# Twelfth slot of a fused top-k attention and gated MLP: diagonal matrices ahead of the last weight roundings, a later output copy, and seven buffers in two pools

## The chip, the cores and the metric

The kernel runs on one core of a Trainium2 chip. The metric is the device time of one launch in microseconds (us), as the median of several runs. Lower is better. The core has five engines with queues of their own: TensorE (PE, with its weight loads listed apart as PEld), VectorE (DVE), ScalarE (ACT), GpSimd (POOL) and SyncE (SP), which here only issues DMAs. Each works through its own list in the order in which the kernel wrote it; semaphores order the engines among each other.

## The reference

```python
# attention: q, k, v of shape (8, 8, 576, 64) = (B, H, S, D), top_k = 32
scores = (1.0 / np.sqrt(D)) * np.matmul(q, k.transpose(0, 1, 3, 2))
kth = np.partition(scores, -top_k, axis=-1)[..., -top_k:-top_k + 1]
scores = np.where(scores >= kth, scores, -1000000000.0)
attn = np.exp(scores - np.max(scores, axis=-1, keepdims=True))
attn = attn / (np.sum(attn, axis=-1, keepdims=True) + 1e-09)
x = np.matmul(attn, v)            # then (B, H, S, D) -> (B*S, H*D) = (4608, 512)
# MLP: w_in (512, 2048), w_out (2048, 512)
h = x @ w_in
g = h * (1.0 / (1.0 + np.exp(-1.702 * h)))
out = g @ w_out
```

The gate is computed as h times (1 + tanh(0.851 h)), with the factor one half applied when the output is copied.

## The kernel before, in words

**Tiles and slots.** A unit of attention is a slot: 128 query rows of two heads. A batch has 18 slots, so 8 batches make 144. Slots 0 to 12 are written one at a time by `slot(n)` (the constant `SETTLED` is 12), from slot 13 on `two_slots(n)` writes two at a time, and `last_slot()` drains what is left of the MLP. All orders are written out by hand under a manual schedule: an engine does what the Python code issued for it, in that order.

**One slot of attention.** `scores(n)` multiplies queries and keys on PE into the tiles `s_ps` (L282). `copy_scores(n)` brings them to SBUF as `sc` on ACT (L294). DVE then searches the 32 largest values of each row: with MAX8 and MATCH_REPLACE8 over 576 columns up to slot 11 (L304, L307), and from slot 12 on in two halves of 288 columns, `greater` and `lesser` (`pair_up`, L323 on DVE, L326 and L327 on POOL; `topk_of_pairs`, L344 to L356), which gives `cut`. `bounds(n)` makes `low` from it on POOL (L377). `exponentials(n)` masks and exponentiates on ACT (L397, L400). Up to slot 11 `divide(n)` then forms 1/sum on DVE (L408, L410) and, on POOL, two diagonal matrices `by` that hold it (L413; they lie in one place of the tensor `xT`). `turn_main` and `turn_ends` multiply the probabilities by these matrices on PE, so that they come out turned and divided (L448, L451), and ACT copies them to `pt` (L456). From slot 12 on ACT splits the probabilities into 16-bit halves (`split`, L470), SP writes them to DRAM (`rows`, L472) and brings them back with a transposing DMA (L478); sums are then divided out later through `wide` (L433) and L527. `values` (L503) or `values_at` (L538) multiplies by v, and ACT copies the result (L516, or `x` at L953 with L552 on POOL after it) to `xT`.

**The MLP beside it.** When 128 rows of `xT` are complete they make a block, and the MLP of the blocks runs in pieces between the attention's steps: `hidden()` multiplies by `win` on PE (L595), `tanh()` takes the hyperbolic tangent on ACT into a tile `th` (L617) and, from slot 13 on, also copies h (tile `h`, L620), `gate()` multiplies the two (on DVE at L632 up to slot 12, on POOL at L629 and L630 afterwards), and `project()` multiplies by `wout` on PE into `po` (L650). A block takes four `project()` calls with four matmul groups each. After the fourth, `leave` copies `po` to a tile `ob` on ACT (L658) and SP writes it out (L660). `project(True)` puts that copy off to the next `leave_all()`. The next block's first L650 has to wait until `ob` has been copied, because `po` is one buffer.

**Weights.** The 32 weight pieces arrive as 64-bit words and are turned into float32 in the first slots ("rounding"). SP loads a piece to a tile `raw` one slot ahead (L126), ACT and DVE prepare it (L151 to L154), and POOL ends it with two operations, L144 and L147. These two go to a list `unfinished` and are issued inside the next slot's search on DVE, by `finish_one()`: the first three after the third operation of the search, all that are left after the sixth, behind `divide`. Slot 11 prepares the last two pieces, so slot 12 issues four such operations.

```python
for i, op in enumerate(topk_of_pairs(n) if n >= PAIRED else topk(n)):
    op()
    if i == 2:
        for _ in range(min(3 if n >= TURNS else 6, len(unfinished))):
            finish_one()
    if i == 5:
        if n > 0:
            divide(n - 1)
        while unfinished:
            finish_one()
```

**Buffers.** The pool `raws` has 8 buffers of 4 KB a partition, and the tiles `raw`, `lesser`, `h`, `x` and `wide` take turns in it. The pool `thp` has 5 buffers of 2 KB, shared by `th` and `ob`. A tile is written only when the last reader of the tile that had the buffer before is done.

**From slot 12 to slot 13.** `slot(12)` ends with `project()` and `hidden()`. `two_slots(13)` (where `opens` is true) then issues `scores(15)`, `bring_all()` with a `hidden()`, `exponentials(12)`, `split(12)`, `copy_scores(15)`, a `tanh`, the search of slot 13, another `hidden`, `project_one()` and a second `tanh`.

Of the kernel before, what the change touches and what calls it, by code (L numbers as in the profile page):

```python
# [30 lines left out]
def kernel(  # L31
# [53 lines left out]
    SETTLED = 12  # L85
# [3 lines left out]

    const = ctx.enter_context(tc.tile_pool(name="const", bufs=1))  # L90
    pool = lambda name, bufs, **kw: ctx.enter_context(tc.tile_pool(name=name, bufs=bufs, **kw))
    raws = pool("raws", 8)
    loads = pool("loads", 2)
    vals = pool("vals", 4)
    qkt = pool("qkt", 6)
# [3 lines left out]
    small = pool("small", 4)  # L99
    ptp = pool("ptp", 2)  # L100
    xs = const.tile([P, 5, CC, P], F32, name="xT")
    thp = pool("thp", 5)
    apart = pool("apart", 4, space=DRAM)
    apart_qk = pool("apart_qk", 2, space=DRAM)
    ps_s = pool("ps_s", 2, space=PSUM)
# [506 lines left out]
    def tanh(aside):  # L612

        if to_gate:
            ph, g, blocks = to_gate.pop(0)
            th = thp.tile([P, G * P], F32, name="th")
            nc.scalar.activation(th[:], ph[:], AF.Tanh, scale=0.851 / RAISE)  # L617
            if aside:
                h = raws.tile([P, G * P], F32, name="h", tag="raw")
                nc.scalar.copy(out=h[:], in_=ph[:])  # L620
                ph = h
            gated.append((th, ph, g, blocks))
# [14 lines left out]
    def project(put_off_leaving=False):  # L637

        gT, fs, blocks = to_project.pop(0)
        for x in blocks:  # L640
            if not x.done:
                home = "ps_h" if "ps_p" in in_use else "ps_p"
                in_use.append(home)
                x.home = home
                pool_of, tag = (ps_h, "ph") if home == "ps_h" else (ps_p, "po")
                x.po = pool_of.tile([P, C], F32, name="po", tag=tag)
        i = 0
        for f in fs:
            for x in blocks:
                nc.tensor.matmul(  # L650
                    x.po[:], lhsT=gT[:, i * P : (i + 1) * P], rhs=wout[:, f, :], start=(x.done == 0), stop=(x.done == FC - 1)
                )
                x.done += 1
                i += 1

        def leave(x):
            ob = thp.tile([P, C], F32, name="ob", tag="th")
            nc.scalar.mul(out=ob[:], in_=x.po[:], mul=0.5 / RAISE**2)  # L658
            for on, to in x.rows:
                nc.sync.dma_start(to, ob[on, :])  # L660

        for x in blocks:
            if x.done == FC:
                in_use.remove(x.home)
                leaving.append(lambda x=x: leave(x))
        if not put_off_leaving:
            leave_all()
# [4 lines left out]
    def leave_all():  # L672
        while leaving:
            leaving.pop(0)()
# [116 lines left out]
    def slot(n):  # L791

        todo = later.pop(n, [])
        for fn, args in todo:
            if fn is not prepare and fn is not prepare_by_dma:
                fn(*args)
        preparing = [(fn, args) for fn, args in todo if fn is prepare or fn is prepare_by_dma]
        some = [round_piece(x) for x in by_slot.get(n, [])] if n else early
        if n == 0:
            for piece in some:  # L800
                piece["low"]()
                piece["sign"]()
        else:
            bounds(n - 1)
            if n == PAIRED:
                pair_up(n)

            exponentials(n - 1, bring_all if n % 4 == 1 else lambda: None)
            copy_scores(n + 1)
            bring_all()  # L810
            while signs:
                signs.pop(0)()
            if 1 < n <= TURNS:
                turn_main(n - 2)
                turn_ends(n - 2)
            for piece in some:
                piece["size"]()
            tanh(False)
        for i, op in enumerate(topk_of_pairs(n) if n >= PAIRED else topk(n)):
            op()  # L820
            if i == 2:
                for _ in range(min(3 if n >= TURNS else 6, len(unfinished))):
                    finish_one()
            if i == 5:
# [4 lines that stand above are left out]
            if i == 10:  # L829
                gate(False)  # L830
        for piece in some:
            piece["shift"]()
            unfinished.extend(piece["finish"])
        if n < NP:
            for fn, args in preparing:
                fn(*args)
        if n >= TURNS:
            turn_main(n - 1)
            turn_ends(n - 1)
        if n > 0:  # L840
            for piece in some:
                piece["low"]()
        scores(n + 2)
        if n == SETTLED:
            copy_scores(n + 2)
        if n == 0:
            return
        for i, piece in enumerate(some):
            if n == TURNS and i > 0:
                signs.append(piece["sign"])  # L850
            else:
                piece["sign"]()
        idle = not ready and n < TURNS
        if 1 < n <= TURNS:
            values(n - 2, put_off if n == TURNS else None)
        if n >= TURNS:
            values(n - 1, put_off)
        if n >= NP:
            for fn, args in preparing:
                fn(*args)  # L860
        if n > PROJECTS and may_project(2):
            project()
        if idle:
            stay_warm(8)
        hidden()
# [12 lines left out]
    def two_slots(n):  # L878

        first, second = [later.pop(m, []) for m in (n, n + 1)]  # L880
        live = lambda m: 0 <= m < N
        aside = n < N

        def begin(todo):
            for fn, args in todo:
                if fn is not prepare and fn is not prepare_by_dma:
                    fn(*args)

        def prepare_some(todo):
            for fn, args in todo:  # L890
                if fn is prepare or fn is prepare_by_dma:
                    fn(*args)

        def find(m):
            for i, op in enumerate(topk_of_pairs(m) if live(m) else [lambda: None] * 23):
                op()
                if i == (13 if m < SETTLED + 4 else 8) and m % 2:
                    invert(m - 2)
                if i > 1 and unfinished:
                    finish_one()  # L900

        def project_one():
            if may_project(0):
                project(True)

        def measure(m):
            if live(m):
                bounds(m)
            gate(aside)

        opens = n == SETTLED + 1
        ahead = n < SETTLED + 4
        begin(first)
        measure(n - 1)
        if ahead:
            scores(n + 2)
        if opens:
            bring_all()
        if live(n - 1):
            exponentials(n - 1)  # L920
            split(n - 1)
        if ahead:
            copy_scores(n + 2)
        if opens:
            tanh(aside)
        find(n)
        hidden(ps_t if opens else None)
        project_one()
        tanh(aside)
        prepare_some(first)  # L930
        held = [m for m in (n - 3, n - 2) if live(m) and "rows" in st[m]]
        o = ps_t.tile([P, 2, 2, P], F32, name="o", tag="tp") if held else None
        for i, m in enumerate(held):
            sum_rows(m, o[:, i, 0, :])
        if live(n + 2) and not ahead:
            scores(n + 2)
            copy_scores(n + 2)
        leave_all()
        for i, m in enumerate(held):
            values_at(m, o[:, i, 1, :])  # L940
        if live(n - 1):
            turn_by_dma(n - 1)
        while turns:
            turns.pop(0)()
        if live(n + 3):
            scores(n + 3)
        begin(second)
        measure(n)
        def bring():
            if not held:  # L950
                return
            x = raws.tile([P, 2, 2, P], F32, name="x", tag="raw")
            nc.scalar.copy(out=x[:], in_=o[:])  # L953
            for i, m in enumerate(held):
                x_of(m, x[:, i, 1, :], x[:, i, 0, :])

        if live(n):
            exponentials(n, bring)
        else:
            bring()  # L960
        if live(n):
            split(n)
            turn_by_dma(n)
        hidden(ps_t)
        if live(n + 3):
            copy_scores(n + 3)
        tanh(aside)
        prepare_some(second)
        project_one()
        leave_all()  # L970
        find(n + 1)
# [39 lines left out]
```

## Time and profile before

| what | value |
|---|---|
| median of 3 runs | 1477.44 us (1475.12 to 1478.23) |
| the profiled execution, its own time | 1475.54 us |
| its span in the profile | 1473.8 us |
| PE busy | 1433.5 us (97%) |
| DVE busy | 1333.4 us (90%) |
| ACT busy | 1173.9 us (80%) |
| POOL busy | 862.9 us (59%) |

The span runs from the first to the last instruction that the profiler saw; some 1.7 us of the execution's own time lie around it. Times of instructions are given from the span's start. A busy PE is modelled, so PE's share says where it has gaps and not how good its work is. In a row of the timeline the columns are start, length, engine, line, operation, output and inputs, shapes and count; a bracket at its end gives the idle time before it and what ended it. A row of waits reads: who waited, for whom, us in total, number of times, longest.

### The profile page before, as it was taken

What the parts mean: (1) busy time and instruction counts of PE and PEld (TensorE: products, weight loads), DVE (VectorE), ACT (ScalarE), POOL (GpSimd) and SP (SyncE); (2) the same over time, 40 slices, a digit from 0 to 9 for tenths busy, and PEclk for the clock granted to TensorE, in tenths of its full rate; (3) what the DMA queues carried; (4) which work ended last, traced back from release to release, by engine and by line L of the source; (5) the groups of instructions that cost most, each with busy time, mean ns of one, the idle gap of its engine ahead of it and who ended that gap; (6) DMA issues with size and microseconds to landing.
All of it is one profiled execution on the core that took longest, in us unless ns stands there. A gap on an engine that the chain in (4) does not pass through costs nothing.

```text
span 1473.8 us, 29103 instructions
## 1 busy us (share of the span) xinstructions
PE 1433.5 (97%) x9696; PEld 1017.8 (69%) x9696; DVE 1333.4 (90%) x4541; ACT 1173.9 (80%) x1865; POOL 862.9 (59%) x1119
## 2 busy tenths in 40 slices
PE   7789899999999999999999999999999999999998
PEld 5667656777666667777666667777666667777665
DVE  7999899999999999999999999999999999999910
ACT  6998687978788887888878787888878788887730
POOL 3777655665666666566665666655666666655510
PEclk8899999999999999999999999999999999999999
DMA  7451256877767677676768686666776766654430
GB/s 244 134 156 55 56 157 180 213 176 177 176 187 198 169 187 188 178 191 162 187 177 204 168 187 184 183 183 170 182 186 185 199 170 187 153 126 128 125 86 15
DMA packets 516311, 242.04 MB, mean 164 GB/s; under 512 B 452672, under 2 KB 490560, under 8 KB 516160
## 3 DMA queue, kind: packets, MB, share of 16 engines
q1 hardware_dynamic: 515728, 239.89, 62.1%
q8 instruction: 76, 1.25, 0.4%
q14 instruction: 75, 0.61, 0.1%
q10 hardware_dynamic: 432, 0.30, 0.1%
HBM read 45.09 MB, written 102.24 MB: 100 GB/s over the span
## 4 chain that ended last, share of the span: by engine, by line
PE 89%; DVE 5%; ACT 3%; issue 2%; DMA 1%; POOL 0%; POOLq 0%; ACTq 0%; SPq 0%
PE ph L595 33%; PE po L650 32%; PE s_ps L282 10%; PE o L538 10%; DVE top L304 3%; DVE left L307 2%; PE tp L448 1%; PE o L527 1%; ACT pr L400 1%; ACT sc L397 0%; ACT sc L294 0%; PE o L503 0%; DMA pt<-rows 0%; PE none L169 0%; DVE win L152 0%
## 5 line engine op out<-in xcount | busy, mean ns | idle before, releaser
L595 PEld LDWEIGHTS ph<-xT,win 128*128 128x128 f32 x3520 | 484.1, 191 | 86.8 <-issue 57.5
L595 PE MATMUL ph<-xT,win 128*128 128x128 f32 (+1 forms) x3520 | 537.6, 309 | 1.4 <-POOL xT L552 1.2
L650 PE MATMUL po<-wout,th 128*128 128x512 f32 x1152 | 518.4, 593 | 1.1 <-ACT ob L658 1.1
L650 PEld LDWEIGHTS po<-wout,th 128*128 128x128 f32 x1152 | 213.2, 190 | 214.5 <-issue 207.4
L344 DVE MAX8 top<-left 128x8 f32<-128x288 f32 x792 | 325.3, 445 | 0.0
L470 ACT COPY sc<-pr 128x2304 uint16<-128x2304 uint16 x132 | 278.8, 2112 | 4.2
L294 ACT ACTIVATE sc<-s_ps 128x576 f32<-128x576 f32 x288 | 171.1, 646 | 137.0 <-PE s_ps L282 133.6
L552 POOL TENSOR_TENSOR xT<-x 128x128 f32<-128x128 f32 (+1 forms) x148 | 60.5, 432 | 296.7 <-ACT x L953 296.7
L347 DVE MATCH_REPLACE8 left<-top,left 128x288 f32<-128x288 f32 x528 | 229.7, 442 | 0.0
L400 ACT ACTIVATE pr<-sc,low 128x576 f32<-128x576 f32 x288 | 221.4, 778 | 0.0
L326 POOL TENSOR_TENSOR lesser<-sc,greater 128x576 int32<-128x576 int32 x132 | 186.4, 1412 | 58.0 <-DVE greater L323 57.3
L344 DVE MAX8 top<-lesser 128x8 f32<-128x288 f32 x528 | 213.7, 445 | 0.0
L397 ACT ACTIVATE sc<-sc,cut 128x576 f32<-128x576 f32 x288 | 208.2, 779 | 3.4 <-POOL cut L388 3.3
L327 POOL TENSOR_TENSOR lesser<-lesser,sc 128x576 int32<-128x576 int32 x132 | 186.6, 1414 | 10.4
L282 PE MATMUL s_ps<-qk_t 64*128 64x288 f32 (+1 forms) x1280 | 183.1, 433 | 0.2 <-ACT qk_t L218 0.2
L630 POOL TENSOR_TENSOR th<-th,h 128x512 f32<-128x512 f32 x128 | 163.7, 1279 | 10.8 <-POOL th L629 0.2
L629 POOL TENSOR_SCALAR th<-th 128x512 f32<-128x512 f32 x128 | 80.0, 625 | 125.4 <-ACT th L617 125.3
L323 DVE TENSOR_TENSOR greater<-sc 128x576 f32<-128x576 f32 x132 | 101.6, 770 | 48.2 <-ACT sc L294 47.5
L538 PE MATMUL o<-pt,v_l 128*64 128x128 f32 (+1 forms) x2368 | 143.6, 265 | 0.2 <-DMA pt<-rows 0.2
L538 PEld LDWEIGHTS o<-pt,v_l 128*64 128x64 f32 x2368 | 119.7, 137 | 25.7 <-issue 22.1
L282 PEld LDWEIGHTS s_ps<-qk_t 64*128 64x128 f32 (+1 forms) x1280 | 99.6, 178 | 41.4 <-issue 22.7
L617 ACT ACTIVATE th<-ph 128x512 f32<-128x512 f32 x144 | 86.0, 597 | 50.8 <-PE ph L595 43.4
(83 smaller groups left out, 1461.6 us busy)
## 6 DMA issues: line engine op xcount, KB each, us to landing
rows<-sc SPq DMA_DIRECT2D x132, 576.0 KB, 3.1
qk_rows<-halves SPq DMA_DIRECT2D x48, 256.0 KB, 2.8
qk_l<-in_q_dram SPq DMA_DIRECT2D x64, 128.0 KB, 3.0
raw<-in_moe_w_in_dram SPq DMA_DIRECT2D x16, 512.0 KB, 4.9
v_l<-in_v_dram SPq DMA_DIRECT2D x32, 256.0 KB, 3.3
raw<-in_moe_w_out_dram SPq DMA_DIRECT2D x16, 512.0 KB, 3.4
out_dram<-ob SPq DMA_DIRECT2D x32, 256.0 KB, 2.8
qk_l<-in_k_dram SPq DMA_DIRECT2D x62, 128.0 KB, 2.8
```

What stands on the lines that cost most here:

```text
L282: nc.tensor.matmul(ps[i][rows, c, 0:HALF], lhsT=qT[b, hps[p]][on, cols], rhs=kT[b, hps[p]][on, FIRST[i] + c * HALF : FIRST[i] + (c + 1) * ...
L294: nc.scalar.mul(out=to, in_=ps[i][:, :, 0:HALF], mul=SCALE)
L326: nc.gpsimd.tensor_tensor(out=whole, in0=a.bitcast(I32), in1=greater[n][:].bitcast(I32), op=ALU.subtract)
L327: nc.gpsimd.tensor_tensor(out=whole, in0=whole, in1=b.bitcast(I32), op=ALU.add)
L344: nc.vector.max(found(r, i, True), src[:, i, :])
L347: nc.vector.match_replace(to[:, i, :], found(r, i), src[:, i, :], LOWEST)
L397: nc.scalar.activation(sc[:, i, :], sc[:, i, :], AF.Prelu, bias=cut[:, i : i + 1], alpha=HUGE)
L400: nc.scalar.activation(pr[:, i * S : (i + 1) * S], sc[:, i, :], AF.Exp, bias=low[:, i : i + 1], accum_out=den[:, i : i + 1],)
L470: nc.scalar.copy(out=halves, in_=pr[:].bitcast(U16).rearrange("p (k h) -> p h k", h=2))
L538: nc.tensor.matmul(o[j * D : (j + 1) * D, cols], lhsT=main[:, j, c, :] if c < NF else tail[:, j, :], rhs=pt[:, MAIN[j] + c if c < NF else ...
L595: nc.tensor.matmul(ph[:, i * many * P : (i + 1) * many * P], lhsT=win[:, c, f * P : (f + 1) * P], rhs=xs[:, first : first + step * (many - ...
L650: nc.tensor.matmul(x.po[:], lhsT=gT[:, i * P : (i + 1) * P], rhs=wout[:, f, :], start=(x.done == 0), stop=(x.done == FC - 1))
```

## The change

Five edits. The pool `raws` gets 7 buffers in place of 8, and `thp` 7 in place of 5, so the SBUF that the two take together stays the same (32 and 10 KB a partition before, 28 and 14 KB after). In slot 12 no rounding operation is issued after the third operation of the search, so all four follow after the sixth, behind `divide(11)` and its two L413. In slot 12 `project()` puts its output copy off. And in `two_slots(13)` a `leave_all()` ahead of the first `tanh` issues that copy, now behind `exponentials(12)`, `split(12)` and `copy_scores(15)`; its DMA (L660) on SP so comes behind the DMA of `rows` for slot 12 (L472). No operation is added or removed, and PE and DVE keep their order.

```diff
-    raws = pool("raws", 8)
+    raws = pool("raws", 7)
...
-    thp = pool("thp", 5)
+    thp = pool("thp", 7)
...
-            if i == 2:
+            if i == 2 and n < SETTLED:
                 for _ in range(min(3 if n >= TURNS else 6, len(unfinished))):
                     finish_one()
...
         if n > PROJECTS and may_project(2):
-            project()
+            project(n == SETTLED)
...
         if opens:
+            leave_all()
             tanh(aside)
```

Lines from L925 on have a number that is higher by one after the change (L953 becomes L954).

## The prediction

> **What bounds the kernel now.** I read the page's shares first, then its slices, then the chain, then the stretch around slot 12 engine by engine.
>
> ```profile
> span 1473.8 us, 29103 instructions
> PE 1433.5 (97%) x9696; PEld 1017.8 (69%) x9696; DVE 1333.4 (90%) x4541; ACT 1173.9 (80%) x1865; POOL 862.9 (59%) x1119
> PE   7789899999999999999999999999999999999998
> PE 89%; DVE 5%; ACT 3%; issue 2%; DMA 1%; POOL 0%; POOLq 0%; ACTq 0%; SPq 0%
> ```
>
> PE is the bound but for the first slices. The table of stretches makes it sharper:
>
> ```profile
> 232.00:1387.00 1155.00, 1154.82 (x7760) 813.45 (x7762) 1100.45 (x3904) 956.63 (x1453) 707.10 (x927) 1.00 0.69 178
> ```
>
> (Columns: stretch, length, busy PE, PEld, DVE, ACT, POOL, granted clock, DMA share, GB/s.) From 232 to 1387 us PE idles 0.18 us, while DVE has 54.6 us to spare. So what ends earlier before 232 us can end the kernel earlier by as much, and gaps elsewhere on PE hardly exist. Up to slot 11 DVE is the bound (9.97 busy in nearly each 10 us); the change hardly touches that part. What is left is the stretch from 146 to 232 us. On PE, POOL and ACT it reads:
>
> ```profile
> 141.34 1.95 PE L448 MATMUL tp<-xT,pr 128*128 128x128 f32 x16
> 145.96 3.84 PE L595 MATMUL ph<-xT,win 128*128 128x128 f32 x32
> 153.58 3.68 PE L448 MATMUL tp<-xT,pr 128*128 128x128 f32 x16 [3.77 <-POOL xT L413]
> 159.97 3.70 PE L650 MATMUL po<-wout,th 128*128 128x512 f32 x8
> ...
> 149.27 1.29 POOL L144 TENSOR_TENSOR wout<-wout,raw 128x512 int32<-128x512 int32 x1
> 150.64 1.28 POOL L147 TENSOR_TENSOR wout<-wout,raw 128x512 f32<-128x512 f32 x1
> 151.88 1.29 POOL L144 TENSOR_TENSOR wout<-wout,raw 128x512 int32<-128x512 int32 x1
> 153.14 1.23 POOL L413 TENSOR_SCALAR xT<-ident,rden 128x128 f32<-128x128 f32 x2
> ...
> 163.71 0.60 ACT L658 ACTIVATE ob<-po 128x512 f32<-128x512 f32 x1 [3.69 <-PE po L650]
> 175.66 0.60 ACT L617 ACTIVATE th<-ph 128x512 f32<-128x512 f32 x1 [4.14 <-PE po L650]
> 176.78 0.66 PE L217 MATMUL tp<-ident,qk_l 128*128 128x128 f32 x4 [0.73 <-ACT h L620]
> ```
>
> PE has nothing from 149.81 to 153.58: it waits for the first diagonal matrix, which stands on POOL behind three roundings. DVE had delivered 1/sum at 149.62 (L410, 149.45 plus 0.17). When PE starts again, L448 takes 3.68 us where slot 11 took 1.95:
>
> ```profile
> 154.00:155.00 1.00, 1.00 (x7) 0.50 0.00 0
> 155.00:156.00 1.00, 1.00 (x6) 0.50 0.00 0
> 157.00:158.00 1.00, 1.00 (x10) 0.98 0.00 0
> ```
>
> (Stretch, length, PE busy, granted clock.) The clock is halved until about 157 us.
>
> **What the Trainium skill says.** "TensorE: Matmul & The Clock Gate", Part 1: The HAM clock gate, has PE fall to half its clock after an idle window of about 3.4 us and recover after about as long a busy one. The trace agrees: 3.77 us idle, then 0.50 for some 3 us; the 1.86 us gap at 224.5 left the clock at 1.00. "SBUF — State Buffer", SBUF: two separate sides, has DVE operations with two SBUF inputs and POOL take turns at a shared port. It fits the second L413 here (883 ns beside a DVE L323, other L413 some 375 ns); I use 0.72 us for the pair, as in slot 10. "Perfetto Trace Analysis", Optimization Strategy, reads the same gap repeating as a lack of buffers; here the th wait comes only three times (4.14, 1.53, 1.22 us, all between 171 and 195 us).
>
> **The change part by part.**
>
> *Roundings behind L413.* POOL ends L327 of slot 12 at 149.32, and would start L413 at 149.8 (1/sum at 149.62 plus the 0.17 us that the same step takes in slot 11: 138.44 to 138.61). The first matrix is there at 150.15, the second at 150.5. PE, free at 149.81, starts L448 at 150.2: gain 153.58 - 150.2 = **3.4 us**. A gap of 0.4 us leaves the clock up, so L448 takes 1.95 instead of 3.68: **1.7 us** more. L451, L282 and L503 follow as in slot 11 (0.3 us of slack for the ACT copies L456 there), and L650 starts near 154.9 instead of 159.97. It is the user of the last two pieces: the four roundings take 5.3 us in sum and end at 150.5 + 5.3 = 155.8 instead of 155.62. Of the four matmul groups (0.9 us each) that start at 154.9, the third reads piece 30 (done by 153.2) and the fourth, at 157.6, piece 31. Price zero, covered by 1.8 us. The next on POOL, L326 for slot 13, is 0.2 us later; DVE reads it at 162.93, 4 us after it is ready.
>
> *Output copy put off.* Now ACT stands 3.69 us for `po` at 160 us with L516, L397, L400 and L470 of slot 12 queued behind. After the change L516 follows values(11) at 155, L397 can go when `cut` is there (DVE L356, 156.9), L400 when `low` is (POOL, about 159.1; now 158.95), so L400 ends at 160.7, L470 at 162.9, L294 of slot 15 at 164.0 and `ob` at **164.5** (lengths 1.5, 2.1, 1.1, 0.6 from the rows now). Who waits for `ob`: PE's next L650, which follows L282 (158.6) and 64 L595 (159.8 to 167.1) and so starts at 167.1 instead of 172.02. Slack 2.6 us, price zero; if the cover were gone it costs what ACT is late. SP: `rows` of slot 12 goes out near 162.9, L660 waits for `ob` to 164.5 behind it, and the transposing L478 waits for `rows` (2.8 us now) to 165.7 anyway. Nothing is delayed there.
>
> *Seven th buffers.* The three waits of ACT L617 for L650 go. Each held `h`, and thereby the PSUM buffers that L217 and L221 need: PE gaps of 0.73 (176.06) and 0.78 us (195.2). Not all of that goes, since L221 waits for the ACT copy of the first half anyway, as it would some 0.2 us without it: **0.5 + 0.6 = 1.1 us**. From ACT's side nothing is late next: it is done with L620 near 168.3, PE needs the buffer at 170.7.
>
> *Seven raw buffers.* SP may load piece i when piece i-7 is rounded, instead of i-8. The trace gives both ends: piece 27 would be loaded at 105.95 instead of 102.31, lands 3.4 us later at 109.4 and is read by L151 at 116.37. Over all pieces the least slack is 6.7 us, also for the v and k loads queued behind on SP. From slot 13 on, a pair of slots takes six buffers (wide, lesser, h, x, h, lesser) in about 19 us; going back seven, the tightest reader is DVE's last read of a `lesser` (254.7), whose buffer the `h` near 264 gets. 9 us of slack, price zero.
>
> **Does the gain last?** Up to 180 us DVE is continuously busy and can't move; its results of slots 12 to 14 (156.9, 165.8, 174.7) come before ACT's new times by 2 us or more except the first, counted above. Then DVE's waits for ACT, 1.14 + 2.85 us at 180 to 184.5 and 1.20 us at 200.5, are what it can give; it moves up 5.2 us. ACT is the bound from 199.5 to 227 (the chain runs through L400, L470, L294, L397 there), and starts when PE has done L538: now 199.5, then 193.3. The cuts of slots 16 to 22 have 2.5 us or more in hand before ACT (slot 19: 227.06 against 229.60), so DVE moving up 1 us less than PE does no harm. L595 starts at 231.93 less 6.2. Behind it PE is full and DVE has about 1 us a pair to spare.
>
> Sum: 3.4 + 1.7 + 1.1 = **6.2 us**; I take 6.0 for small waits not seen. The span would be 1467.8 and that execution 1475.54 - 6.0 = 1469.5. The median of runs lies 1.9 us above that execution, so 1477.44 - 6.0 = **1471.4**.
>
> **Bounds of what is not shown.** L413 with port conflict: 0.4 us later. No warm clock: 1.7 lost. Waits of th not the cause of the PE gaps: 1.1 lost; gone whole: 0.4 gained. Some ACT slack gained in 157 to 199 us could also shorten ACT's own stretch: up to 1.4 us more gain (its wait at 198.1). Gain from 3 to 8 us.
>
> **Rivals.**
> - *The put-off copy becomes the wait.* If slot 12's exponentials keep their place at 164.35 (because POOL gives `low` late), `ob` ends at 171.0, L650 waits from 167.1, and 3.9 of 6.3 us are given back: gain 2.4, 1475.0. Against it: `low` of slot 12 comes at 158.95 even now.
> - *The lead is eaten.* ACT is 91% busy and DVE 94% between 199 and 232 us; if either sets its own start, the gain is 0 to 1 us: 1477. Against it: `x` (L953) at 199.52 waits 1.37 us for PE, and DVE has 5.2 us of waits before.
> - *Weights come late: slower.* One raw buffer fewer delays each third piece. It decides if a piece takes over 10 us (3.4 median and 6.7 slack; the longest of the trace was 8.3 to land). Then ACT, and DVE behind it, wait in slots 3 to 11, say 2 us in nine slots: 18 - 6 = 12 us slower, 1489. For it: SP already waits 19 times for roundings.
> - That the change doesn't act is hard to hold: in the built order both L413 stand directly behind L327, ahead of all four roundings, and `ob` behind L294.
>
> **Numbers.** Full gain 0.80, copy as wait 0.10, lead eaten 0.06, late weights 0.04. About 0.2% (3 us) can be told from no change. The first case is faster but for its lower edge (0.79), the second and third mostly within 0.2% (0.16), the last slower; I put 0.05 there for noise too. The likeliest alone is 1469.5 to 1473; the range of eight in ten, with the bounds and the second case, is 1469.0 to 1475.0.
>
> **What would show it.** In the profile after: L448 of slot 12 starts near 150.2 and takes 2 us, PE clock 1.00 there; L658 of slot 12 behind L470 near 164; no L617 waiting for L650; the first L595 after the b=1 pairs near 226 instead of 232; PE still without gaps behind it. I am wrong if PE waits for `ob` near 167, if SP holds a weight past its L151, or if gaps come after 226 us that take the lead back.

## Result, and the profile after

The changed kernel takes 1469.42 us (median of 4 runs, 1468.78 to 1470.06) against 1477.84 us before: ratio 0.9947, interval 0.993 to 0.9964, that is 7.8 us less by the ratio (5.3 to 10.3). A second comparison of the same two kernels gave 0.9962 (0.995 to 0.9975), 5.6 us less (3.7 to 7.4). The forecast was 6.0 us less, a median of 1471.4 us in a range of 1469.0 to 1475.0; the measured median stands near the lower edge of that range. The profiled execution took 1468.81 us, its span 1467.0.

Page of the kernel after: span, busy time, PE in 40 slices.

```profile
span 1467.0 us, 29219 instructions
PE 1430.7 (98%) x9696; PEld 1015.8 (69%) x9696; DVE 1336.3 (91%) x4541; ACT 1173.9 (80%) x1865; POOL 863.1 (59%) x1119
PE   7789989999999999999999999999999999999998
```

Timeline of the kernel after, PE, around slot 12 and at the head of PE's full stretch:

```profile
149.77 2.05 PE L448 MATMUL tp<-xT,pr 128*128 128x128 f32 x16 [1.24 <-POOL xT L413]
154.53 3.70 PE L650 MATMUL po<-wout,th 128*128 128x512 f32 x8
171.29 0.33 PE L221 MATMUL tp<-ident,qk_l 128*128 128x128 f32 x1 [0.24 <-ACT qk_t L218]
198.88 3.70 PE L650 MATMUL po<-wout,th 128*128 128x512 f32 x8 [1.13 <-ACT ob L658]
225.40 3.84 PE L595 MATMUL ph<-xT,win 128*128 128x128 f32 x32
```

The wait for the first diagonal matrix is 1.24 us instead of 3.77, L448 takes 2.05 us instead of 3.68, and the first L595 behind the attention-only stretch stands at 225.4 instead of 231.9. The same times on POOL and ACT:

```profile
149.34 0.72 POOL L413 TENSOR_SCALAR xT<-ident,rden 128x128 f32<-128x128 f32 x2 [0.54 <-DVE rden L410]
150.03 1.29 POOL L144 TENSOR_TENSOR wout<-wout,raw 128x512 int32<-128x512 int32 x1
```

```profile
163.59 0.60 ACT L658 ACTIVATE ob<-po 128x512 f32<-128x512 f32 x1
166.78 0.60 ACT L617 ACTIVATE th<-ph 128x512 f32<-128x512 f32 x1 [1.63 <-PE ph L595]
```

L413 now waits for DVE's 1/sum and no longer for roundings. `ob` is copied by 164.2, 2.4 us before PE's L650 at 166.58 needs `po` free, and L617 waits for its input, not for a th buffer. Table of stretches, after (in the second row the stretch of the same length that was shown of before):

```profile
154.00:155.00 1.00, 1.00 (x13) 0.66 (x10) 1.00 (x3) 0.85 (x3) 0.98 (x1) 1.00 0.00 0
226.00:1381.00 1155.00, 1154.85 (x7766) 813.25 (x7766) 1104.31 (x3909) 956.12 (x1452) 706.49 (x925) 1.00 0.69 178
```

The clock is whole, and PE stays full behind 226 us: instructions that were at 294 us and later all stand 6.71 us earlier, up to the last output copy (6.72).

Part of the 6.7 us is chance. In the profiled execution of before the clock was also halved in slot 8, where the change does nothing; in that of after it was not:

```profile
106.00:108.00 2.00, 2.00 (x11) 0.50 0.43 117
```

```profile
106.00:108.00 2.00, 2.00 (x19) 1.00 0.33 68
```

(Stretch, length, PE busy, clock, DMA share, GB/s; first before, then after.) In the execution of after PE then stands 1.27 us earlier in slot 11, and DVE's 1/sum for slot 12's matrices comes 0.45 us earlier (149.17 against 149.62). Less that, the profile shows some 6.3 us, an estimate.

### The profile page after: what moved, and what is told of

The parts are those of the page before. It is cut to its first block, busy times and chain, and to the rows that moved or that the text cites. A ratio compares the mean times of both kernels' runs of the same rounds, so it can differ in the third digit from the quotient of the medians.

```text
span 1467.0 us, 29219 instructions
## 1 busy us (share of the span) xinstructions
PE 1430.7 (98%) x9696; PEld 1015.8 (69%) x9696; DVE 1336.3 (91%) x4541; ACT 1173.9 (80%) x1865; POOL 863.1 (59%) x1119
## 4 chain that ended last, share of the span: by engine, by line
PE 82%; DVE 13%; ACT 2%; issue 1%; DMA 1%; SPq 1%; POOL 0%; POOLq 0%; DVEq 0%; ACTq 0%
PE ph L595 31%; PE po L650 30%; PE o L538 10%; PE s_ps L282 10%; DVE top L304 4%; DVE left L307 3%; DVE top L344 2%; DVE left L347 1%; PE o L527 1%; DMA rows<-sc 1%; DVE greater L323 0%; DMA pt<-rows 0%; DVE lesser L347 0%; DVE th L632 0%; ACT pr L400 0%
## 5 line engine op out<-in xcount | busy, mean ns | idle before, releaser
L595 PEld LDWEIGHTS ph<-xT,win 128*128 128x128 f32 x3520 | 484.1, 191 | 86.9 <-issue 57.4
L595 PE MATMUL ph<-xT,win 128*128 128x128 f32 (+1 forms) x3520 | 537.6, 309 | 1.4 <-POOL xT L552 1.2
L650 PE MATMUL po<-wout,th 128*128 128x512 f32 x1152 | 518.4, 593 | 1.1 <-ACT ob L658 1.1
L650 PEld LDWEIGHTS po<-wout,th 128*128 128x128 f32 x1152 | 213.2, 190 | 214.5 <-issue 207.1
L538 PE MATMUL o<-pt,v_l 128*64 128x128 f32 (+1 forms) x2368 | 143.5, 264 | 0.1
L538 PEld LDWEIGHTS o<-pt,v_l 128*64 128x64 f32 x2368 | 119.7, 137 | 25.5 <-issue 23.5
L617 ACT ACTIVATE th<-ph 128x512 f32<-128x512 f32 x144 | 85.9, 597 | 43.8 <-PE ph L595 40.8
```

Source lines behind the costliest of these rows:

```text
L538: nc.tensor.matmul(o[j * D : (j + 1) * D, cols], lhsT=main[:, j, c, :] if c < NF else tail[:, j, :], rhs=pt[:, MAIN[j] + c if c < NF else ...
L595: nc.tensor.matmul(ph[:, i * many * P : (i + 1) * many * P], lhsT=win[:, c, f * P : (f + 1) * P], rhs=xs[:, first : first + step * (many - ...
L650: nc.tensor.matmul(x.po[:], lhsT=gT[:, i * P : (i + 1) * P], rhs=wout[:, f, :], start=(x.done == 0), stop=(x.done == FC - 1))
```

## Experiments

Each group of kernels shares its runs of the kernel before. The medians of the kernels with early roundings lie between 1467.7 and 1470.7 us and the intervals are some 4 us wide, so differences among these kernels are read from the trace as well.

| kernel | median us | before us | ratio | interval |
|---|---|---|---|---|
| roundings only | 1469.83 | 1476.14 | 0.9966 | 0.9953 to 0.998 |
| buffers only | 1475.58 | 1476.14 | 0.9994 | 0.9985 to 1.0002 |
| late copy only | 1475.25 | 1476.14 | 0.9993 | 0.9985 to 1.0002 |
| before, stall filled | 1473.09 | 1476.14 | 0.9981 | 0.9974 to 0.9989 |
| whole change again | 1470.34 | 1475.49 | 0.9962 | 0.995 to 0.9975 |
| roundings only again | 1469.29 | 1475.49 | 0.9956 | 0.9943 to 0.9968 |
| no late copy | 1470.70 | 1475.49 | 0.9965 | 0.9951 to 0.9979 |
| no buffers | 1469.74 | 1475.49 | 0.9962 | 0.9949 to 0.9974 |
| change, later gaps filled | 1469.03 | 1476.81 | 0.9951 | 0.9939 to 0.9964 |
| the same, no buffers | 1469.09 | 1476.81 | 0.9953 | 0.9939 to 0.9966 |
| change, split later | 1467.66 | 1476.81 | 0.9946 | 0.9933 to 0.9958 |
| change, five raw buffers | 1469.46 | 1475.50 | 0.9957 | 0.9944 to 0.9971 |

**1. Roundings alone.**

```diff
-            if i == 2:
+            if i == 2 and n < SETTLED:
```

> Of the change only the order of the last four roundings (behind L413 in slot 12); 8 raw and 5 th buffers, output copy at once. Theory (PE's stall and the cold clock behind it are worth 3.4 + 1.7 us and last to the end): L448 of slot 12 starts near 150 us, takes 2.0 us, the clock stays at 1.00, and the time is 5 us below the kernel before; L617 still waits three times for L650. Rival (another engine sets the pace before 232 us and eats the lead): L448 is early, but L595 of the first block after the gap starts within 1 us of 231.9, and the time is that of the kernel before.

Five of six runs were 1469.2 to 1470.5, so this edit alone brings what the whole change brings. The sixth, the profiled one, took 1475.2: it had the lead at 200 us (4.9 us) and lost 4.6 us of it later, in one place, seen on PE's timeline and in the table of stretches (stretch, length, PE busy, clock, DMA share, GB/s):

```profile
150.28 2.05 PE L448 MATMUL tp<-xT,pr 128*128 128x128 f32 x16 [1.18 <-POOL xT L413]
200.48 3.70 PE L650 MATMUL po<-wout,th 128*128 128x512 f32 x8 [1.13 <-ACT ob L658]
247.26 1.09 PE L538 MATMUL o<-pt,v_l 128*64 128x128 f32 x16 [3.18 <-DMA pt<-rows]
```

```profile
248.00:252.00 4.00, 4.00 (x26) 0.59 0.75 186
```

PE waited 3.18 us for a transposing DMA, and the clock halved behind it. About half of the wait is the transfer itself, which took 6.34 us to land (4.78 in the same place before). The other half is its start: it was issued 3.2 us ahead of PE's need, against 4.6 us before, and why it was late is not shown. The margin there is small in the other kernels too (before waited 0.18 us at 249.0, after had 0.6 us in hand), so they may meet the same.

**2. Buffers alone.**

```diff
-    raws = pool("raws", 8)
+    raws = pool("raws", 7)
...
-    thp = pool("thp", 5)
+    thp = pool("thp", 7)
```

> Of the change only the buffers: 7 raw, 7 th. Theory: the three waits of L617 for L650 are gone, PE's gaps of 0.73 and 0.78 us shrink to some 0.25 each, the lead is 1.1 us. Rival a (the gaps are then filled by the next wait): no change. Rival b (one raw buffer fewer delays weights): slower by 1 us or more, with L151 waiting for a load. PE's 3.8 us stall in slot 12 and the halved clock stay.

No change that can be told (0.9994), but the interval reaches from 2.2 us faster to 0.3 us slower, so neither 0 nor the 1.1 us of the theory is excluded. In its trace the L617 waits for L650 are gone and PE's gaps at L221 are 0.24 us each; L151 waits for a load three times, 1.1 us in all (twice, 0.9 us, before). So the mechanism acts, and this comparison can't tell what it is worth.

**3. Late copy alone.** (`project(n == SETTLED)` and the `leave_all()`.)

> Of the change only the put-off output copy, with the old order of roundings and 8 and 5 buffers. Theory: ACT no longer idles 3.7 us for po, exponentials of slot 12 start near 160.5 instead of 164.35, but nothing on PE waits for them: 0 us, within 0.3. Rival (ACT's lead brings DVE and so the later scores forward): faster by 1 to 3 us. Rival (po's next user waits for the late copy): slower by up to 3 us, with L650 waiting for L658 near 172.

No change that can be told (0.9993). PE's stall (4.03 us) and the gaps of 0.73 and 0.78 us are there. `ob`, now issued later, makes L617 wait 2.4 us for its DMA under five th buffers, without a gap on PE.

**4. The stall filled.**

```diff
+        if n == SETTLED:
+            idle_tile = ps_t.tile([P, 512], F32, name="fill", tag="tp")
+            for _ in range(14):
+                nc.tensor.matmul(idle_tile[:, 0:P], lhsT=ident[:], rhs=ident[:], start=True, stop=True)
         if n >= TURNS:
             turn_main(n - 1)
```

> The kernel before with 14 matmuls of the identity put ahead of L448 in slot 12, into a PSUM tile that nobody reads, so that PE is busy in its stall (14 x 2 passes of 0.12 us, some 3.4 us). The stall for L413 stays. Theory (L448 takes 3.68 us because the clock halves after the idle stretch): L448 starts where it did, near 153.6, takes about 2.0 us, clock 1.00, and the kernel is 1.7 us faster though it does more work. Rival (L448 is slow because of its operands or of the ACT copies behind it): no change, or slower by what the filler overruns.

PE does more work and the kernel is 2.8 us faster (ratio; 1.6 to 3.8). On PE's timeline:

```profile
148.57 3.29 PE L840 MATMUL fill<-ident 128*128 128x128 f32 x28
152.74 2.05 PE L448 MATMUL tp<-xT,pr 128*128 128x128 f32 x16 [0.88 <-POOL xT L413]
```

L448 starts no earlier than the matrix allows and takes 2.05 us. So its slowness was the clock. The size is at the high end: the traces price the halving at 1.4 us (buffers only), 1.6 (before) and 2.8 (late copy only), read as PE's time from L448 of slot 12 to the L650 that waits for `ob` near 200 us, less the same in a kernel with the same buffers and whole clock (50.53 less 49.11; 51.83 and 52.99 less 50.20). How long the clock stays down differs by execution. Table of stretches of the late copy alone, PE:

```profile
152.00:154.00 2.00, 1.30 (x6) 0.50 0.00 0
154.00:156.00 2.00, 2.00 (x11) 0.50 0.00 0
156.00:158.00 2.00, 2.00 (x11) 0.50 0.00 0
158.00:160.00 2.00, 2.00 (x24) 0.83 0.00 0
```

With the slices on either side this adds up to 6.8 us at half clock; in the profiles of before and of the buffers alone the same sum gives 3.4 us. PE can lose half of such a time, 3.4 or 1.7 us, and lost 2.8 and 1.6 or 1.4. The mean granted clock of the runs fits the size that was measured: it is 0.9887 over the 36 runs of before and 0.9907 over the 14 of this kernel, and 0.0020 of 1474 us is 2.9 us of clock, an estimate.

**5. The whole change and its parts on one chip.**

> The changed kernel itself, as the mark for the three others of this group: 1469.4 us, some 6.7 us below the kernel before, L448 of slot 12 near 150 us, no L617 waiting for L650.

> Of the change only the order of the last four roundings, as in the first group, now beside the whole change on one chip. Theory (seven th buffers give 1.1 us that last): 1.1 us slower than the whole change. Rival (what the buffers give before 200 us is taken back by a wait further on, for instance of L538 for a transposing DMA near 245 us, which cost 3.2 us in the first profile of this kernel): within 0.3 us of the whole change.

> The change without the put-off copy: roundings behind L413 and 7 and 7 buffers, L658 issued at once in slot 12. Theory (the put-off copy has price and gain zero, since ACT has slack until 193 us): ACT idles 3.7 us for po again, the time is that of the whole change within 0.3 us. Rival (ACT's exponentials of slot 12 then hold up PE): 0.5 to 2 us slower than the whole change, with PE waiting for ACT between 160 and 180 us.

> The change without the buffers: roundings behind L413 and the put-off copy with 8 raw and 5 th buffers. Theory: the three waits of L617 for L650 are back, PE's gaps of 0.73 and 0.78 us with them, 1.1 us slower than the whole change. Rival (those gaps are absorbed later): within 0.3 us of it. A second rival: with the late copy the five th buffers make a fourth wait (L617 for the DMA of ob, 2.4 us in the copy-only kernel), which reaches PE: 2 us slower or more.

Medians 1470.3, 1469.3, 1470.7 and 1469.7: the two kernels without the new buffers are not slower. The trace says more. From L448 of slot 12 to the L650 near 200 us PE takes 49.11 or 49.12 us in both kernels with 7 th buffers and 50.20 in both with 5: the buffers give 1.09 us there. From that L650 to the span's end it is 1269.6 (whole change), 1269.4 (no late copy), 1269.5 (roundings) and 1268.2 us (no buffers); it was 1268.1 in the first profile of the change. Three of the four lost over 1 us behind 218 us. Table of stretches of the whole change, PE alone:

```profile
218.00:222.00 4.00, 1.90 (x10) 0.85 0.83 166
222.00:226.00 4.00, 4.00 (x48) 0.72 0.64 161
```

The clock falls around PE's gap of 1.85 us at L221 in slot 19, in three of these executions (not in that without the buffers) and in that of the late copy alone, and not in others. The late copy makes no difference that can be told. In the kernel without the new buffers L617 does wait a fourth time, 3.57 us for the DMA of `ob`, but PE has no gap from it, so the second rival fell.

**6. The later gaps filled, with and without the buffers.**

```diff
+        for _ in range(keep_busy[0] if name == "k" else 0):
+            nc.tensor.matmul(
+                last_ps[0][:, 1, HALF : HALF + P], lhsT=ident[:], rhs=ident[:], start=True, stop=True
+            )
         if name == "k":
...
+    last_ps, keep_busy = [None], [0]
...
+        last_ps[0] = ps[0]
...
+        keep_busy[0] = {17: 3, 19: 7}.get(n, 0)
         prepare_some(first)
+        keep_busy[0] = 0
```

> The whole change, with 3 and 7 matmuls of the identity put into PE's gaps of 0.89 and 1.86 us in the pairs of slots 17 and 19 (ahead of L221, into columns of a scores tile that nobody reads). Three of six profiles with early roundings show the clock at about half for 2 to 3 us behind the second gap, 1.1 to 1.6 us lost. Theory (that halving, met in some executions only, takes back what the th buffers gave): the clock stays at 1.00 from 150 us on in every execution, the spread of the runs shrinks and the median falls 0.5 to 1 us below that of the change (1469.4 to 1470.3). Rival (the halving has nothing to do with the gap, or the filler delays L221): no change or slower by up to 1 us.

> The same filler in the kernel with early roundings and late copy but 8 raw and 5 th buffers. With the halving out of the way the buffers' own worth can be read. Theory (the gaps of 0.73 and 0.78 us last to the end): 1.1 us slower than the filled kernel with 7 and 7 buffers. Rival (something else takes it back, the transposing DMA near 245 us for one): within 0.3 us.

The clock is whole in both profiles:

```profile
218.00:222.00 4.00, 3.44 (x28) 1.00 0.77 154
222.00:226.00 4.00, 4.00 (x55) 1.00 0.58 144
```

The stretch from the L650 near 200 us to the end takes 1267.8 us in both, as long as in the kernel with only slot 12's stall filled (also 1267.8), whose clock was whole behind 200 us without this filler. The runs of the filled change span 1.2 us. Its median of 1469.03 is below both medians of the unfilled change (1469.42 and 1470.34), but these come from other groups and the intervals overlap, so a gain can't be told. The filled kernel without the buffers was to be 1.1 us slower and is not: 1469.09. In the two profiles the kernel with the buffers came to L448 of slot 12 1.0 us later (150.31 against 149.31), which cancels its 1.06 us behind that. This late arrival is not the buffers' rule: over the profiles with early roundings slot 12's L448 starts at 149.9 on average with 7 and 7 buffers (five kernels) and at 149.8 with 8 and 5 (four).

What takes the buffers' 1.1 us back in the medians is not shown. The granted clocks point one way: in the group of experiment 5 the ten runs with 7 th buffers (whole change, no late copy) have 0.9897 on average, the ten with 5 (roundings, no buffers) 0.9908, and 0.0011 of 1468 us is 1.6 us of clock, an estimate. But single runs scatter by as much as 0.002, the first comparison's four runs of the change also have 0.9908, and where the clock fell in the runs without a profile is not recorded. So the cause stays open.

**7. ACT's split later in slots 17 and 19**, aimed at PE's remaining gaps.

```diff
             exponentials(n - 1)
-            split(n - 1)
+            if n not in (17, 19):
+                split(n - 1)
...
         prepare_some(first)
+        if n in (17, 19):
+            split(n - 1)
```

> The whole change, and in the pairs of slots 17 and 19 ACT's split (L470, 2.1 us) behind the copies L218 to L224, so that PE does not wait for these. Theory (ACT idles 1.38 us twice for the scores in this stretch and can use it): PE's gaps of 0.89 and 1.86 us shrink to 0.25, L294 comes 0.4 and 1.2 us earlier, the kernel is 1.2 us faster than the change, and with no long gap the clock stays up. Rival (the rows that leave 1.6 us later make their transposing DMA late for L538): no gain, or slower by up to 3 us, with PE waiting for pt near 240 us.

1467.66 us, the lowest of all medians; its group's filled change had 1469.03, and the two intervals overlap. Timeline, PE:

```profile
217.43 0.33 PE L221 MATMUL tp<-ident,qk_l 128*128 128x128 f32 x1 [0.24 <-ACT qk_t L218]
221.36 1.09 PE L538 MATMUL o<-pt,v_l 128*64 128x128 f32 x16 [0.53 <-DMA pt<-rows]
241.18 1.09 PE L538 MATMUL o<-pt,v_l 128*64 128x128 f32 x16 [0.36 <-DMA pt<-rows]
```

Both gaps at L221 shrink to 0.24 us (the line shows the second), and the rival's wait is there too: L538 now waits 0.53 and 0.36 us for the later DMA. From the L650 near 200 us to the end it takes 1267.1 us, 0.7 less than the filled kernels and 1.0 less than the change in its first profile; the theory had 1.2.

**8. Five raw buffers** (`pool("raws", 5)` in place of 7).

> The whole change with 5 raw buffers in place of 7, to find where the weights' slack ends. Piece i may then be loaded only when piece i-5 is rounded: by the trace of the change piece 24 at 102.5, landing near 106.0 against L151 at 104.97, piece 27 near 117.4 against 116.5, piece 21 near 94.4 against 93.7. Theory (slack was 6.7 us with 7 buffers and is spent with 5): L151 waits up to 1 us for the third piece of slots 5 to 9 and the kernel is 0.5 to 3 us slower than the change. Rival (ACT takes these waits without DVE noticing): within 0.3 us of the change (1469.4 to 1470.3), though L151 waits.

1469.46 us: the rival. Waits:

```profile
ACT win L151 <- DMA raw<-in_moe_w_in_dram: 2.6, 5, 0.7
ACT wout L151 <- DMA raw<-in_moe_w_out_dram: 1.1, 2, 0.7
```

ACT waits 3.7 us in seven places, 0.40 us of it for piece 24, which L151 then reads at 106.16, and the time does not show it. Two buffers fewer than the change has cost nothing that can be measured.

## Why the prediction was right

- **Roundings behind L413, 3.4 us.** Right in kind and size. Counted from DVE's 1/sum of slot 11 (the start of L410), L448 of slot 12 starts 15.0 to 15.3 us later in the four profiles with the old order and 11.7 to 12.0 us later in the ten with the new one, on average 3.4 us less. L413 starts at 149.34 (149.8 forecast), L448 at 149.77 (150.2). PE's wait was 1.24 us and not 0.4, because PE came 1.27 us earlier and the matrix only 0.45; the clock held all the same. Wout's last piece ends at 155.70 (155.8 forecast) and no L650 waits.
- **The clock, 1.7 us.** Right in kind, shown by the filler. The size was too small for the median: it came from one execution with a short drop, where three executions show 1.4, 1.6 and 2.8 us and the filler is worth 2.8 (1.6 to 3.8). With it the roundings alone bring 5.0 us (2.9 to 6.9) and 6.5 us (4.7 to 8.4) in two comparisons, where the sum had 5.1.
- **Late copy, 0.** Right: `ob` at 163.6 (164.5 forecast), L650 at 166.6 (167.1), alone 0.9993, left out 0.4 us within the noise. The rival that it becomes the wait fell.
- **Seven th buffers, 1.1 us.** The one step that is not found in the time. The gaps went as forecast, 1.09 us by 200 us. But three pairs of kernels that differ in the buffers alone show 1.41, 0.60 and -0.06 us more for having them (no late copy against roundings, the change against no buffers, and the filled two). That the 1.86 us gap in slot 19 leaves the clock at 1.00, and that gaps "hardly exist" on PE behind 232 us, was read from one execution; others have a halved clock around that gap or a late DMA at 247 us, each of the size of this step or more. In two profiles with the buffers the halved clock took it; what does so elsewhere is not shown.
- **Seven raw buffers, 0.** Right, with slack to spare at five.
- **The lead lasts.** Right: 6.5 us at 199 us, 6.71 from 294 us to the end. DVE's waits of 1.14, 2.85 and 1.20 us were given up as said, and ACT carried the lead through 193 to 225 us. The lead-eaten and late-weights rivals fell.
- **The sum, 6.2 us, in part by luck.** The clock was worth about 1 us more in the median than its term, and the buffers' 1.1 us were not found, so two errors cancel. The median of 1471.4 was 2 us too high for another reason: it carried over the 1.9 us by which the median of before lay above its profiled execution, without asking where they come from. Behind the change the median lies only 0.6 us above the profiled execution. In the 63 runs of before in the experiments the time goes with the granted clock (1478.3 us on average at 0.986, 1473.5 at 0.992), so an offset of this size goes with clock drops, and the change takes the one behind slot 12's stall away.

## What to carry to other kernels

Where one engine is full for most of the run, look for the last stall before it fills: here a gap there was worth its whole length to the end, and the slow clock behind it besides. Small operations on a critical path (two diagonals of 0.37 us each) should stand ahead of bulk work on a shared queue, whatever the bulk work's age. A gain of a microsecond or less read from one profile needs the spread of several: clock drops and late DMAs of that size come and go between executions.

## What was not expected of the hardware

The clock also drops around gaps well below the 3.77 us of slot 12: with gaps of 1.85 and 0.25 us (PE busy 1.90 of 4 us) its mean over the next 4 us was 0.57 to 0.72 in four profiles, and 1.00 behind the same gaps in seven others. In slot 8 it was halved behind a gap of 2.56 us in the profile of before and whole behind one of 2.62 us in that of after. 28 matmul instructions whose result nobody reads, put into a stall, made the kernel 2.8 us faster.

A long operation on POOL can hold up a very small one on DVE. With the old order L408, which adds a constant to 128x2 values, took 1.26 to 1.31 us in three of four profiles, where it started with or just behind POOL's L144 (0.06 us at most) and ended 0.03 us behind it; in the profile of before it started 0.03 us ahead of L144 and took 0.17 us, as in all ten profiles with the new order. From the late copy alone:

```profile
148.47 1.26 DVE L408 TENSOR_SCALAR some<-den 128x2 f32<-128x2 f32 x1 [0.59 <-ACT pr L400]
148.41 1.29 POOL L144 TENSOR_TENSOR wout<-wout,raw 128x512 int32<-128x512 int32 x1
```

The new order so also spares DVE 1.1 us in such executions. PE's start of L448 did not depend on it: under the old order it comes 15.0 to 15.3 us behind slot 11's 1/sum with this delay and 15.3 us without it (before).
